# Weight conversions beside the first attention units are queued behind the exponentials of their unit, and the copies of transposes and outputs are ranked higher

## Chip, core and metric

The kernel runs on one core of a Trainium2 chip. The metric is the device time of one launch in microseconds: the median over several executions. One execution was also taken with the hardware profiler; all rows below come from it.

## What is computed

The reference, cut to what matters: a windowed attention with sink columns over 2 batches and 8 heads of 64, and then two feed-forward layers of width 2048 over the 1536 tokens.

```
scores = scale * q @ k.T                      # (2, 8, 768, 768)
keep   = (pos < n_sink) | (0 <= rel < window) # n_sink 4, window 128
a      = softmax(where(keep, scores, -1e9))
x      = (a @ v) as 1536 x 512
h = x @ w_in  (512 x 2048);  g = relu(h)**2;  x = g @ w_out (2048 x 512)
h = x @ w_in2;  P = a0 + a1*h + a2*h^2 + a3*h^3
Q = 1 + |b0|*|h| + |b1|*h^2;  g = P/(Q + 1e-6);  out = g @ w_out2
```

## The kernel before

**Groups and units.** The tokens are cut into four groups (`GROUPS`): 512, 256, 256 and 512 tokens. The attention of a group consists of units, one for each pair of heads and each segment of two blocks of 128 tokens. Group 0 has eight units, called 0 to 7 here. Even ones hold the first two blocks of the batch (score widths 128 and 256), odd ones blocks 2 and 3 (width 288 with the sink columns). A unit (`att_unit`) runs in these steps: scores on TensorE into PSUM banks (L300); on VectorE (DVE) mask and row minimum (L306); on ScalarE (ACT) the exponential with its sum (L308); on DVE one over the sum (L311, L312); normalisation of the first block on GpSimd (POOL) and of the second on DVE (L316); transposes of the normalised probabilities on TensorE (L333); their copies to SBUF, `pT` of head 0 on ACT and of head 1 on DVE (L335); in odd units also the copy `pS` of the sink columns on ACT (L347); the products with v (L356, L368); and the output, `xhi` on ACT (L374) and `xlo` on DVE (L375).

**Conversions.** Weights come as 64-bit floats. One conversion (`wconv`, which calls `w_split`) takes one block of 128x512 from a staging buffer `st` (three buffers): ACT casts `top` (L133), DVE joins it with the middle bits into `wt` (L134), ACT rounds `whi` (L419), DVE subtracts `wlo` (L420). It then asks for the next `st` load on SP's queue (L124). Conversions are numbered from 1 here, in the order of the list `lq`. Numbers 1 to 4 are the w_in blocks f = 0 to 3, 5 is w_out block 0, 6 is w_in block 4, 7 is w_out block 1, and then w_in and w_out blocks alternate.

**The loop of group 0.** In `run`, iteration k of the first loop traces the scores, exponentials and normalisation of unit k, then the transposes and copies of unit k-1, then `CONV[k]` conversions, then (for k = 3, 5, 7) six matmuls of the first layer for blocks f = 0 and 1 (`gemm1_part`, L435 to L437), then the products with v and the output of unit k-1. After the loop the first layer of group 0 runs over all 16 blocks f: `gemm1` (L435 to L437), `act1` on ACT (L444 to L446) and DVE (`glo`, L447), `gemm2a` (L458, L459, L464). Between them stand slots in which the units of group 1 advance (`tick`), and further conversions.

**What sets the order.** TensorE's order in these parts is the order in which the code is written (`manual_schedule`). The other engines and SP's queue are ordered by the framework's scheduler at build time, by priority and its own timeline; on the chip every engine then runs its list from front to back. `tc.issue_after(ins)` puts an instruction behind `ins` on its engine; `tc.high_priority(offset=...)` raises the priority of what is traced inside. `lastV` and `lastA` are the latest mask step and exponential traced by `att_unit`.

Of the kernel before, what the change touches and what calls it, by code (L numbers as in the profile page):

```python
# [37 lines left out]
YEVAC_ACT = (0, 1)  # L38
PINNED = (0, 1, 2)
NUNIT = (4, 4, 8)  # L40
CONV = (1, 1, 1, 1, 1, 1, 1, 1, 1)
PER = 5
HEAD = 2
DEPTH = 4
# [2 lines left out]
LAG2 = 3  # L47
TAIL = 3
HP = 60
NTOP = 1  # L50
IAD = 3
ST_T = 5
# [9 lines left out]
def seg_dims(seg):  # L62

    _, blk0, nb = seg
    pv = 1 if blk0 > 0 else 0
    wk = 2 * nb * P + NSK if pv else nb * P
    wq = nb * P
    nkb = nb + pv  # L70
    return wk, wq, nkb, nkb * P, (2 * nb * D if pv else 0)
# [55 lines left out]
def to_f32(nc, st, t, top):  # L127

    mid = st.bitcast(I32)[:, 1 : 1 + 2 * WH].rearrange("p (n w) -> p n w", w=2)[:, :, 0]
    head = st.bitcast(BF16)[:, 4 : 4 + 4 * WH].rearrange("p (n w) -> p n w", w=4)[:, :, 0]
    nc.scalar.copy(top.bitcast(F16).rearrange("p (n w) -> p n w", w=2)[:, :, 1], head)  # L133
    nc.vector.scalar_tensor_tensor(t.bitcast(I32), in0=mid, scalar=13, in1=top,  # L134
                                   op0=ALU.logical_shift_right, op1=ALU.bitwise_or)
# [20 lines left out]
class Fast:  # L156
# [17 lines left out]
    def setup(self):  # L174
        nc, c = self.nc, self.const
        self.zero = c.tile([P, P], BF16, name="zero")
        nc.gpsimd.memset(self.zero, 0.0)
        self.tops = [c.tile([P, WH], I32, name=f"top{i}") for i in range(NTOP)]
        self.conv_i = 0
# [231 lines left out]
    def w_split_(self, which, f, half):  # L411
        nc = self.nc
        st = self.wst.pop((which, f, half))
        t = self.stage.tile([P, WH], F32, tag="wt", name="wt", bufs=2)
        to_f32(nc, st, t, self.tops[self.conv_i % NTOP])
        self.conv_i += 1
# [83 lines left out]
    def run(self, ctx):  # L500
        tc, nc = self.tc, self.nc
# [25 lines left out]
        for u in us:  # L527
            self.att_off[u] = off
            wk, wq, _, wv, wsk = seg_dims(u[2])
# [5 lines left out]
        def prefetch():  # L535
            nonlocal nload
            if nload < len(us):
                g0 = us[nload][0] == 0
                early = (None, 0, 1, 2)[nload % DEPTH] if g0 else None
                u, alt = us[nload], nload % NALT if g0 else 0  # L540
                raws = [self.att_load(u, early, alt), None, None]
                if g0:
                    raws[1] = self.att_load_v(u, alt, 0)
                    if seg_dims(u[2])[4]:
                        raws[2] = self.att_load_v(u, alt, 1)
                loaded.append((u, raws))
                nload += 1
# [7 lines left out]
        def tick():  # L555
            with ExitStack() as c:
                if urgent:
                    c.enter_context(tc.high_priority(offset=HP))
                tick_()
            self.va_hist.append((self.lastV, self.lastA))  # L560

        def tick_():
            nonlocal done, tick_no, ui
            if tick_no % PER == 0 and loaded:
                u, raws = loaded.pop(0)
                g = u[0]
                if g not in self.x32 and g > 0:
                    self.new_x32(g)
                a = self.att_unit(u, raws, ui % NALT if g == 0 else 0)
                ui += 1  # L570
                next(a)
                new = True
            else:
                new = False
            for b in list(active)[::-1]:
                if next(b, "end") == "end":
                    active.remove(b)
                    done += 1
            if new:
                active.append(a)  # L580
                if not loaded:
                    prefetch()
            tick_no += 1
# [15 lines left out]
        cq = [list(lq[0]), list(lq[1])]  # L599
        lq0 = [(f, k) for _, f, k in lq[0]]  # L600

        def wload(which, k=1):
            for _ in range(k):
                if lq[which]:
                    self.w_load(*lq[which].pop(0))

        def wconv(which, f, half):
            if (which, f, half) in self.w:
                return
            assert cq[which].pop(0) == (which, f, half)  # L610
            self.w_split(which, f, half)
            wload(which)
# [14 lines left out]
        g0 = [None] * (n0 + 1)  # L627
        with tc.manual_schedule(engines={mybir.EngineType.PE}):
            for k in range(n0 + 1):
                if k == 0:  # L630
                    wload(0, 3)
                if k < n0:
                    u, raws = loaded.pop(0)
                    g0[k] = self.att_unit(u, raws, k % NALT)
                    for _ in range(3):
                        next(g0[k])
                if k:
                    next(g0[k - 1])
                for _ in range(CONV[k]):
                    wconv(*cq[0][0])  # L640
                while k >= 2 and pc < (k - 1) // per:
                    for f in range(HEAD):
                        self.gemm1_part(0, f, pc, self.x[0], GN[0], hb[f])
                    pc += 1
                if k:
                    next(g0[k - 1])
                while nload < n0 and len(loaded) < DEPTH - 1 or not loaded:
                    prefetch()
            done = n0
# [369 lines left out]
```

## Time and profile before

| | |
|---|---|
| median of 3 runs | 667.8 us (667.75 to 669.43) |
| the profiled execution's own time | 668.77 us |
| its span in the trace | 667.0 us |
| TensorE busy in the span | 632.6 us (95%) |
| DVE, ACT, POOL busy | 423.0, 428.4, 110.6 us |
| bytes moved by DMA | 52.39 MB |

The span is the stretch from the first to the last record; the time of the execution is 1.8 us longer. Busy time of TensorE counts matmuls as the profile models them. Times below are microseconds from the start of the span, unless marked ns.

### The profile page before, as it was taken

To read this page: it belongs to the slowest core of one execution; us is meant where nothing else is said; L and a number is where in the kernel's file an instruction comes from. 1 tells how busy PE (TensorE), PEld (TensorE's weight loads), DVE (VectorE), ACT (ScalarE), POOL (GpSimd) and SP (SyncE) were. 2 spreads that over 40 slices of the span, in tenths; PEclk is the share of its full clock that TensorE was granted. 3 is DMA by queue.
4 is the path that set the end of the run, shared out by engine and by line. 5 is a ranking of instruction groups with operands and counts; after the bars stand their busy time and mean duration, and the time that the engine had idled before them with its cause. 6 is when DMAs were issued, how large, how long until landed. Compare 5 with 4: busy or idle time off the path is not lost.

```text
span 667.0 us, 9984 instructions
## 1 busy us (share of the span) xinstructions
PE 632.6 (95%) x3681; PEld 514.7 (77%) x3681; DVE 423.0 (63%) x849; ACT 428.4 (64%) x912; POOL 110.6 (17%) x122
## 2 busy tenths in 40 slices
PE   5678999999999999999999999999999999999994
PEld 2455667777888878899888888888888888888883
DVE  5864687543333444415566649999788887877771
ACT  4854787665545555536677758778686666766661
POOL 2111010000000011103000002354233332222221
PEclk9879999999999999999999999999999999999998
DMA  7940376432111222100556620000010000100001
GB/s 285 316 163 1 130 229 200 161 118 88 34 49 50 70 67 79 31 9 14 172 194 194 195 85 2 0 1 0 1 64 0 1 0 1 57 7 2 0 1 68
DMA packets 20794, 52.39 MB, mean 79 GB/s; under 512 B 2688, under 2 KB 8064, under 8 KB 20736
## 3 DMA queue, kind: packets, MB, share of 16 engines
q1 hardware_dynamic: 20160, 51.52, 23.4%
q8 instruction: 31, 0.51, 0.3%
q14 instruction: 27, 0.22, 0.1%
q10 hardware_dynamic: 576, 0.14, 0.1%
HBM read 48.50 MB, written 3.15 MB: 77 GB/s over the span
## 4 chain that ended last, share of the span: by engine, by line
PE 89%; ACT 4%; DVE 3%; issue 1%; DMA 1%; POOL 0%; POOLq 0%; DVEq 0%
PE b L435 13%; PE b L436 13%; PE b L437 13%; PE b L458 7%; PE b L464 7%; PE b L496 7%; PE b L497 7%; PE b L495 7%; PE b L459 6%; PE b L300 3%; PE b L368 3%; PE b L333 2%; ACT p L308 2%; PE b L356 1%; DVE wt L134 1%
## 5 line engine op out<-in xcount | busy, mean ns | idle before, releaser
L435 PE MATMUL b<-xhi,whi 128*128 128x512 f32 (+1 forms) x320 | 113.4, 355 | 0.5 <-ACT xhi L374 0.5
L437 PE MATMUL b<-xhi,wlo 128*128 128x512 f32 (+1 forms) x320 | 111.0, 347 | 0.0
L436 PE MATMUL b<-xlo,whi 128*128 128x512 f32 (+1 forms) x320 | 110.9, 347 | 0.0
L458 PE MATMUL b<-ghi,whi 128*128 128x512 f32 (+1 forms) x256 | 84.9, 348 | 0.7 <-ACT ghi L445 0.7
L459 PE MATMUL b<-ghi,wlo 128*128 128x512 f32 (+1 forms) x256 | 81.9, 336 | 0.0
L486 POOL TENSOR_TENSOR glo<-t,ghi 128x512 fp32r<-128x512 f32 x34 | 45.0, 1323 | 213.3 <-ACT ghi L485 195.3
L496 PE MATMUL b<-wlo,ghi 128*128 128x512 f32 x192 | 74.7, 389 | 0.0
L495 PE MATMUL b<-whi,ghi 128*128 128x512 f32 x192 | 74.4, 389 | 0.0
L447 DVE TENSOR_TENSOR glo<-b,ghi 128x512 fp32r<-128x512 f32 (+1 forms) x64 | 35.6, 557 | 59.5 <-ACT b L446 58.9
L497 PE MATMUL b<-whi,glo 128*128 128x512 f32 x192 | 71.9, 389 | 0.0
L306 DVE CUSTOM_DVE_ANT_0 p<-b,m 128x288 f32<-128x288 f32 (+2 forms) x96 | 37.0, 419 | 54.7 <-PE b L300 54.7
L435 PEld LDWEIGHTS b<-xhi,whi 128*128 128x128 f32 x320 | 60.3, 189 | 11.9 <-issue 3.8
L308 ACT ACTIVATE p<-p,mn 128x288 f32<-128x288 f32 (+2 forms) x96 | 48.0, 501 | 33.4 <-DVE mn L306 32.9
L316 POOL TENSOR_SCALAR p<-p,sums 128x288 f32<-128x288 f32 (+1 forms) x48 | 27.1, 576 | 253.4 <-DVE sums L312 191.1
L437 PEld LDWEIGHTS b<-xhi,wlo 128*128 128x128 f32 x320 | 60.4, 189 | 7.6
L436 PEld LDWEIGHTS b<-xlo,whi 128*128 128x128 f32 x320 | 60.5, 189 | 7.3
L420 DVE TENSOR_TENSOR wlo<-wt,whi 128x512 fp32r<-128x512 f32 x64 | 45.0, 703 | 27.6 <-ACT whi L419 27.3
L419 ACT CAST whi<-wt 128x512 fp32r<-128x512 f32 x64 | 39.6, 618 | 34.5 <-PE b L436 20.9
L458 PEld LDWEIGHTS b<-ghi,whi 128*128 128x128 f32 x256 | 48.4, 189 | 12.5 <-issue 6.3
L444 ACT ACTIVATE b<-b 128x512 f32<-128x512 f32 (+1 forms) x64 | 31.0, 486 | 41.1 <-PE b L437 41.1
L464 PE MATMUL b<-glo,whi 128*128 128x512 f32 (+1 forms) x256 | 56.6, 343 | 0.0
L134 DVE SCALAR_TENSOR_TENSOR wt<-st,top 128x512 int32<-128x512 int32 x64 | 47.4, 741 | 7.5 <-ACT top L133 5.7
(126 smaller groups left out, 1287.9 us busy)
## 6 DMA issues: line engine op xcount, KB each, us to landing
st<-w SPq DMA_DIRECT2D x64, 512.0 KB, 4.1
raw<-att SPq DMA_DIRECT2D x12, 400.0 KB, 3.3
rawv<-att SPq DMA_DIRECT2D x16, 192.0 KB, 2.9
raws<-att SPq DMA_DIRECT2D x16, 128.0 KB, 2.0
out<-o SPq DMA_DIRECT2D x8, 256.0 KB, 2.0
raw_e<-att SPq DMA_DIRECT2D x4, 400.0 KB, 5.5
raw<-att SPq DMA_DIRECT2D x6, 256.0 KB, 3.4
rawv<-att SPq DMA_DIRECT2D x8, 128.0 KB, 3.9
```

Source lines behind the costliest of these rows:

```text
L134: nc.vector.scalar_tensor_tensor(t.bitcast(I32), in0=mid, scalar=13, in1=top, op0=ALU.logical_shift_right, op1=ALU.bitwise_or)
L308: self.lastA = A.activation(p, p, AF.Exp, scale=-1.0, bias=mn, accum_out=sums[:, k * nb + i : k * nb + i + 1])
L420: nc.vector.tensor_tensor(wlo, t, whi.bitcast(F32), op=ALU.subtract)
L435: nc.tensor.matmul(h[:, :n], whi[:, cs], xhi[:, c, :n], start=(c == 0), stop=False)
L436: nc.tensor.matmul(h[:, :n], whi[:, cs], xlo[:, c, :n], start=False, stop=False)
L437: nc.tensor.matmul(h[:, :n], wlo[:, cs], xhi[:, c, :n], start=False, stop=(c == NC - 1))
L458: nc.tensor.matmul(acc[m], whi[:, ms], ghi, start=(f == 0 and not pk), stop=pk, **kw)
L459: nc.tensor.matmul(acc[m], wlo[:, ms], ghi, start=False, stop=pk, **kw)
L464: nc.tensor.matmul(acc[m], whi[:, ms], glo, start=False, stop=pk or f == NF - 1, **kw)
L495: nc.tensor.matmul(acc[t], ghi[:, ts_], whi, start=(f == 0), stop=False)
L496: nc.tensor.matmul(acc[t], ghi[:, ts_], wlo, start=False, stop=False)
L497: nc.tensor.matmul(acc[t], glo[:, ts_], whi, start=False, stop=(f == NF - 1))
```

## The change

`CONV` holds the number of conversions of iterations 0 to 8. Seven instead of nine are traced in the loop, the two others follow later in the list. They are traced at the end of the iteration, after the output of unit k-1, and each of their instructions is queued behind the mask step or the exponential last traced on its engine, which is that of unit k. The transposes, copies, products with v and outputs of unit k-1 are traced with the priority raised by `HP0`. In the changed kernel the lines of these functions have a number that is one higher (L308 becomes L309).

```
-CONV = (1, 1, 1, 1, 1, 1, 1, 1, 1)
+CONV = (1, 1, 0, 1, 0, 1, 0, 1, 2)
...
+HP0 = 120
...
                 if k:
-                    next(g0[k - 1])
-                for _ in range(CONV[k]):
-                    wconv(*cq[0][0])
+                    with tc.high_priority(offset=HP0):
+                        next(g0[k - 1])
                 while k >= 2 and pc < (k - 1) // per:
                     for f in range(HEAD):
                         self.gemm1_part(0, f, pc, self.x[0], GN[0], hb[f])
                     pc += 1
                 if k:
-                    next(g0[k - 1])
+                    with tc.high_priority(offset=HP0):
+                        next(g0[k - 1])
+                with ExitStack() as cc:
+                    cc.enter_context(tc.issue_after(self.lastV.ins))
+                    cc.enter_context(tc.issue_after(self.lastA.ins))
+                    for _ in range(CONV[k]):
+                        wconv(*cq[0][0])
```

The order of instructions on TensorE and POOL is the same in both kernels; on ACT, DVE and SP's queue it differs up to the end of the first layer of group 0. Three places follow.

The first is ACT's list in the kernel before, from the third conversion to the output of unit 1; the exponentials (L308) of widths 128 and 256 are those of unit 2, `pT`, `pS` and `xhi` belong to unit 1.

```order
L133 CAST top_102<-st 128x512
L308 ACTIVATE p,sums<-p,mn 128x128 x2
L419 CAST whi<-wt 128x512
L308 ACTIVATE p,sums<-p,mn 128x256 x2
L335 COPY pT_289<-b_284 128x512
L133 CAST top_102<-st 128x512
L347 COPY pS<-b_298 128x256
L419 CAST whi<-wt 128x512
L133 CAST top_102<-st 128x512
L419 CAST whi<-wt 128x512
L133 CAST top_102<-st 128x512
L374 CAST xhi<-b_298 128x256
```

This is the same place on ACT in the changed kernel, down to the third conversion's first cast.

```order
L309 ACTIVATE p,sums<-p,mn 128x128 x2
L309 ACTIVATE p,sums<-p,mn 128x256 x2
L336 COPY pT_289<-b_284 128x512
L348 COPY pS<-b_298 128x256
L375 CAST xhi<-b_298 128x256
L309 ACTIVATE p,sums<-p,mn 128x288 x4
L134 CAST top_102<-st 128x512
```

Four `top` and three `whi` casts that stood ahead of the output of unit 1 are gone from there; the first one now follows the exponentials of unit 3.

The second place is DVE's list in the kernel before, from the last mask step of unit 3 (`b_343`) to the first of unit 4 (`b_398`); `pT_368` is unit 2's.

```order
L306 ISA p,mn<-b_343,m_127 128x288
L306 ISA mn 128x1
L420 TENSOR_TENSOR wlo<-wt,whi 128x512
L134 SCALAR_TENSOR_TENSOR wt<-st,top_102 128x512
L335 COPY pT_368<-b_364 128x384
L311 TENSOR_SCALAR sums<-sums 128x4
L312 RECIPROCAL sums<-sums 128x4
L316 TENSOR_SCALAR p<-p,sums 128x288 x2
L420 TENSOR_TENSOR wlo<-wt,whi 128x512
L134 SCALAR_TENSOR_TENSOR wt<-st,top_102 128x512
L420 TENSOR_TENSOR wlo<-wt,whi 128x512
L306 ISA p,mn<-b_398,m_125 128x128
```

In the changed kernel the same stretch of DVE runs from `b_334` to `b_389`, and unit 2's output (`xlo`) is shown behind it.

```order
L307 ISA p,mn<-b_334,m_127 128x288
L307 ISA mn 128x1
L312 TENSOR_SCALAR sums<-sums 128x4
L313 RECIPROCAL sums<-sums 128x4
L336 COPY pT_359<-b_355 128x384
L317 TENSOR_SCALAR p<-p,sums 128x288 x2
L135 SCALAR_TENSOR_TENSOR wt<-st,top_102 128x512
L421 TENSOR_TENSOR wlo<-wt,whi 128x512
L307 ISA p,mn<-b_389,m_125 128x128
L307 ISA mn 128x1
L376 TENSOR_TENSOR xlo<-b_361,xhi 128x256
```

One whole conversion (the third) stands there in place of parts of three, between unit 3's normalisation and unit 4's first mask step.

The third place is ACT's list in the kernel before at the start of the first layer: `xhi` of unit 7, then the activations of the blocks f = 0, 1 and 2 (`b_149`, `b_150`, `b_725`), then the exponentials of the first unit of group 1 and the tenth conversion.

```order
L374 CAST xhi<-b_678 128x256
L444 ACTIVATE b_149<-b_149 128x512
L444 ACTIVATE b_150<-b_150 128x512
L445 ACTIVATE ghi<-b_149 128x512
L446 ACTIVATE b_149<-b_149 128x512
L444 ACTIVATE b_725<-b_725 128x512
L445 ACTIVATE ghi<-b_150 128x512
L446 ACTIVATE b_150<-b_150 128x512
L445 ACTIVATE ghi<-b_725 128x512
L446 ACTIVATE b_725<-b_725 128x512
L308 ACTIVATE p,sums<-p,mn 128x288 x2
L133 CAST top_102<-st 128x512
```

The same start on ACT in the changed kernel; the casts are those of the conversions 7, 8 and 9.

```order
L375 CAST xhi<-b_651 128x256
L420 CAST whi<-wt 128x512
L134 CAST top_102<-st 128x512
L445 ACTIVATE b_149<-b_149 128x512
L445 ACTIVATE b_150<-b_150 128x512
L446 ACTIVATE ghi<-b_149 128x512
L447 ACTIVATE b_149<-b_149 128x512
L420 CAST whi<-wt 128x512
L134 CAST top_102<-st 128x512
L445 ACTIVATE b_725<-b_725 128x512
L446 ACTIVATE ghi<-b_150 128x512
L447 ACTIVATE b_150<-b_150 128x512
```

In the stretch behind it, ahead of the exponentials of group 1's first unit, `whi` of conversion 9 and all of conversion 10 follow, so that ten conversions stand ahead of those exponentials instead of nine. The conversions 4, 5 and 6 stand behind the exponentials of the units 5 and 7 and around the copies of unit 7.

## Rows read from the trace of the kernel before

**Rows 1.** Busy time by stretch; columns as in its header.

```profile
core 0: us, PE busy (x) PEld busy (x) DVE busy (x) ACT busy (x) POOL busy (x), PEclk, DMA share, GB/s
...
16.30:43.10 26.80, 17.56 (x132) 12.03 (x132) 21.61 (x61) 19.34 (x49) 3.44 (x7) 0.75 0.82 288
43.10:63.50 20.40, 17.07 (x160) 11.77 (x158) 11.62 (x45) 10.65 (x35) 3.04 (x6) 1.00 0.08 21
...
92.00:150.00 58.00, 58.00 (x332) 43.54 (x333) 35.66 (x82) 41.51 (x90) 4.90 (x6) 1.00 0.52 170
```

**Rows 2.** Timeline of TensorE, 16 to 44 us; waits in brackets.

```profile
22.34 1.04 PE L356 MATMUL b<-pS,raws 128*64 128x128 f32 x8 [2.71 <-ACT pS L347]
23.17 1.92 PE L368 MATMUL b<-pT,rawv 128*64 128x128 f32 x12
25.02 1.60 PE L300 MATMUL b<-raw_e 64*64 64x288 f32 x16
28.07 0.84 PE L333 MATMUL b<-ident,p 128*128 128x128 f32 x6 [1.45 <-DVE xlo L375]
...
32.25 1.13 PE L368 MATMUL b<-pT,rawv 128*64 128x256 f32 x8 [1.94 <-ACT pT L335]
...
37.55 1.94 PE L333 MATMUL b<-ident,p 128*128 128x128 f32 x8 [2.68 <-DVE xlo L375]
...
43.08 1.20 PE L300 MATMUL b<-raw_e 64*64 64x288 f32 x16
```

**Rows 3.** Timeline of ACT, 16 to 30 us.

```profile
21.94 0.35 ACT L347 COPY pS<-b 128x256 f32<-128x256 f32 x1
...
23.66 0.77 ACT L133 CAST top<-st 128x512 f16<-128x512 bf16 x1
...
25.71 0.78 ACT L133 CAST top<-st 128x512 f16<-128x512 bf16 x1
```

**Rows 4.** Groups by line over the whole span: the four steps of a conversion.

```profile
L133 ACT CAST top<-st 128x512 f16<-128x512 bf16 x64 | 49.5, 774 | 1.2 <-DVE wt L134 1.2
...
L134 DVE SCALAR_TENSOR_TENSOR wt<-st,top 128x512 int32<-128x512 int32 x64 | 47.4, 741 | 7.5 <-ACT top L133 5.7
L420 DVE TENSOR_TENSOR wlo<-wt,whi 128x512 fp32r<-128x512 f32 x64 | 45.0, 703 | 27.6 <-ACT whi L419 27.3
L419 ACT CAST whi<-wt 128x512 fp32r<-128x512 f32 x64 | 39.6, 618 | 34.5 <-PE b L436 20.9 <-DVE wt L134 13.5
```

**Rows 5.** Busy time by stretch, cut where the granted clock changes.

```profile
22.90:26.10 3.20, 3.20 (x30) 2.10 (x30) 1.83 (x4) 2.20 (x4) 0.00 (x0) 0.53 0.57 186
...
33.10:43.20 10.10, 6.96 (x54) 4.89 (x54) 6.59 (x20) 5.31 (x16) 1.85 (x3) 0.51 0.67 238
43.40:63.50 20.10, 16.77 (x158) 11.56 (x150) 11.62 (x45) 10.45 (x35) 3.04 (x6) 1.00 0.08 21
```

**Rows 6.** Timeline of all engines, 42 to 58 us.

```profile
46.01 0.46 ACT L335 COPY pT<-b 128x384 f32<-128x384 f32 x1
...
46.52 0.87 PE L368 MATMUL b<-pT,rawv 128*64 128x256 f32 x8
...
48.27 0.27 DVE L306 CUSTOM_DVE_ANT_0 p<-b,m 128x128 f32<-128x128 f32 x1
...
49.04 1.06 PE L333 MATMUL b<-ident,p 128*128 128x128 f32 x8 [0.83 <-DVE xlo L375]
...
52.85 1.20 PE L300 MATMUL b<-raw_e 64*64 64x288 f32 x16
```

**Rows 7.** Timeline of ACT, 57 to 72 us.

```profile
63.02 0.37 ACT L374 CAST xhi<-b 128x256 fp32r<-128x256 f32 x1 [3.13 <-PE b L368]
64.90 1.07 ACT L444 ACTIVATE b<-b 128x512 f32<-128x512 f32 x2 [1.51 <-PE b L437]
...
71.59 0.54 ACT L308 ACTIVATE p<-p,mn 128x288 f32<-128x288 f32 x1 [2.14 <-DVE mn L306]
```

**Rows 8.** Timeline of TensorE, 57 to 93 us.

```profile
70.23 0.72 PE L300 MATMUL b<-raw 64*64 64x288 f32 x8 [1.60 <-DVE glo L447]
...
90.28 0.70 PE L300 MATMUL b<-raw 64*64 64x288 f32 x4 [1.03 <-DVE mn L306]
```

## The prediction, made before the changed kernel ran

> **What bounds the kernel now.** I first cut the span into stretches by busy time [rows 1]. From 92 us on, as far as that table goes, TensorE is busy without a gap (58.00 of 58.00 us), and TensorE's share over the whole span is 95%. Its order is unchanged, so what the change can win must come from the beginning, where TensorE waits: in 16.3 to 43.1 us it is busy for 17.56 of 26.80 us, and in 43.1 to 63.5 for 17.07 of 20.40 [rows 1]. Every microsecond by which the first layer starts earlier is then handed on to the end, because nothing behind it but TensorE's own work decides.
>
> Next I read TensorE's timeline in the worse stretch [rows 2]. Four waits stand there: 2.71 us for `pS` of unit 1, 1.45 for its `xlo`, 1.94 for `pT` of unit 2, 2.68 for the `xlo` of unit 2, together 8.8. All are for small attention results of ACT and DVE. (Transposes wait for an `xlo` because they take over the PSUM bank that it reads.) ACT's list shows what stands ahead of these results: casts of conversions, which come every 2.05 us (23.66 and 25.71) [rows 3]. That is the period of a chain that goes back and forth: `top` 0.77 us on ACT, `wt` 0.74 on DVE, `whi` 0.62 on ACT, with `wlo` 0.70 on DVE beside the next one [rows 4]. Each step waits for the other engine, and attention queued behind it waits as well. Nine conversions are done before 38 us, none between there and the start of the first layer.
>
> So this trace holds both cases. The scores of the odd units 3, 5 and 7 begin at 25.02, 43.08 [rows 2] and 52.85 [rows 6]. With conversions in between, a pair of units takes 18.06 us; without, 9.77. The clock takes part: it is at the 1.2 GHz level from 22.9 to 26.1 and from 33.1 to 43.2 (granted 0.53 and 0.51), and at 2.4 GHz from 43.4 to 63.5, where TensorE is busy for 16.77 of 20.10 us [rows 5]. Ahead of each fall TensorE had mostly waited.
>
> **The change, part by part.** I work in stages, each ending at the scores of an odd unit; times are estimates from the rows.
>
> A, to the scores of unit 3. Conversion 2 stays where it is. Ahead of `pS` of unit 1 two `top` casts and one `whi` go: 2 x 0.77 + 0.62 = 2.2 us of ACT [rows 4]. Not all of it comes through: DVE's copy of unit 1's transposes is needed too, and it now stands behind unit 2's normalisation, in place of behind two half conversions. I let the products with `pT` start at 21.7 instead of 23.17 [rows 2], so 1.5 us (bounds 1.0 and 2.2). They took 1.92 us at half clock; at full clock I estimate half of that, which saves another 0.9 (bounds 0 and 0.9). Sum 2.4, and unit 3's scores start at 22.6.
>
> B, from unit 3's scores to unit 5's. The base is the pair without conversions, 9.77 us, at full clock. In it the next even unit's first mask step comes 48.27 - 43.08 = 5.19 us after the scores [rows 2, 6]. Conversion 3 is added, and by DVE's list it stands whole between unit 3's normalisation and unit 4's first mask step: `wt`, wait for `whi`, `wlo` is 0.74 + 0.62 + 0.70 = 2.06 us [rows 4]. Against it, `pT` of unit 2 (0.46 us, [rows 6]) no longer sits between the exponentials, so the normalisation comes about 0.4 earlier. Unit 4's mask steps, the `xlo` of unit 2 and with it unit 3's transposes are thus late by 1.7 us. The first cast, `top` (0.77), and the fourth exponential delay `pT` of unit 2 and hence its products with v (46.52 in the row) by about a microsecond; this lies inside the 1.7. Estimate 11.5 us instead of 18.06: 6.6 won. Bounds: 9.8 if the conversion is hidden, 14 if the clock falls again; so 4.1 to 8.3.
>
> C, from unit 5's scores to unit 7's. Conversion 4 is split: only `wt` (0.74) stands ahead of unit 6's mask steps, `wlo` ahead of the last of them. Unit 5's transposes had 0.83 us of wait [rows 6], all for the `xlo` that `wt` now delays, but `pS` of unit 5 moves ahead of the last exponential. I take 0.4 lost (bounds 0 and 1.4, the two steps of DVE).
>
> D, unit 7 to the first activation. Conversions 5, 6 and 7 and the first cast of 8 come here. ACT has idle time for them: 3.13 us ahead of `xhi` of unit 7 and 1.51 ahead of the first activation [rows 7]. `whi` 7 and `top` 8 need 0.62 + 0.77 = 1.39, under 1.51. Cost 0; if that cover were gone it would be 1.4.
>
> E, start of the first layer. `whi` 8 and `top` 9 now stand between the activations of f = 0 and f = 2. The next scores wait for `glo` of f = 2, since they take its bank (1.60 us in 70.23's row, [rows 8]), so this delay is on TensorE's path: I take 1.2 of the 1.39 us (bounds 0 and 2.8, two pairs of casts). The casts behind (`whi` 9, conversion 10) fall in ACT's next gap of 2.14 us [rows 7].
>
> F, until TensorE runs without gaps. Once conversion 10 is through, the list is one conversion ahead of the one before, and the later 1.03 us of wait at 90.28 [rows 8] may go or double. I take 0 (plus or minus 1).
>
> Loads: an `st` load waits until its buffer's conversion has been read, three conversions ahead. The DMA engines are nearly idle from 43.1 to 63.5 (21 GB/s [rows 1]). In the changed order the loads from the seventh on follow the conversions 4, 5, ..., several microseconds before they are read. I cost SP's new order at nothing; the units' own loads move earlier past the `st` loads. The raised priority costs nothing either, and gains only what is counted above.
>
> Sum: 2.4 + 6.6 - 0.4 - 0 - 1.2 + 0 = 7.4 us. The profiled execution took 668.77 us, which becomes 661.4. It lies 0.97 us above the median of the runs shown, so for the median: 667.8 - 7.4 = **660.4 us**.
>
> One rule is weighed here. The rows show the clock at the lower level for 13 us, each time after TensorE had waited much [rows 5]. The Trainium skill ("TensorE: Matmul & The Clock Gate", part 1) says that half rate is the array's default and that only activity releases it. That speaks against counting on full clock in A and B, because the changed stretch still has waits of over a microsecond. By my rows the sum is 7.4 us; by the rule read strictly it would be about 4 (first rival).
>
> **Rivals.**
>
> 1. The clock stays low in A and B. Place: the waits that stage B still has, for `pT` of unit 2 and for unit 4's late mask steps. Price: 0.9 in A and 2.5 in B (11.5 becomes 14): 7.4 - 3.4 = 4.0, so 663.8. For it: TensorE fell twice there before. Against it: it held the upper level from 43.4 to 63.5 with waits of 0.83 [rows 5, 6], and conversion 3 adds only 1.7 us.
>
> 2. The conversions are only moved: the first layer needs 5, 6, 7, 4 in turn, and if TensorE waits there for whole conversions, each exposed one costs 2.05 us [rows 3]. Of 5 to 10, three exposed ones take 6.2 of 7.4 us: 666.6, within the noise. From 3.6 exposed ones on, the kernel is slower than before; with all six it is 12.3 us, thus 672.7. For it: ACT and DVE are the busier ones at that start. Against it: conversion 5 is done some 6 us and 7 some 10 us before their matmuls, by D.
>
> 3. Conversions 3 and 4 hide entirely and the later waits vanish: stage B takes 9.8, C costs 0, E about 0, F gains 1. Then 2.4 + 8.3 + 1 = 11.7, so 656.1. For it: in the pair without conversions DVE is busy 11.62 of 20.40 us [rows 1], so there is room. Against it: DVE's list puts conversion 3 exactly where unit 4 waits.
>
> 4. The change does not do what it says: the scheduler leaves the lists as they were, and the time is 667.8. The lists differ as shown, so this gets next to nothing.
>
> **How the numbers follow.** My own case (gains of 5.5 to 9.5, 658.3 to 662.3) gets 0.58; rival 1 (gains of 2 to 5.5) 0.17; rival 3 (over 9.5) 0.10; rival 2 within 2.0 us of no change, 0.08, and slower 0.06; rival 4, 0.01. About 0.3%, or 2.0 us, is what a measurement of this kernel tells from no change. Faster: 0.58 + 0.17 + 0.10 = 0.85; same 0.08 + 0.01 = 0.09; slower 0.06. The range takes most of rivals 1 and 3: 657.4 to 665.4. The likeliest case's own range is 658.3 to 662.3.
>
> **What would show it.** In the changed profile unit 3's scores should begin near 22.6 us, unit 5's near 34, unit 7's near 44, the first activation near 56.5; granted clock 1.00 from 22 to 44; TensorE's waits for `pS` and `xlo` of units 1 and 2 each under 1.5 us. The scores of group 1's first unit should wait for `glo` some 1.2 us longer than 1.60. I would be wrong if the first activation comes before 53 or after 60, if a `top` cast waits for an `st` load, or if TensorE has gaps beyond about 85 us that it did not have.

## The result, and the profile after

| | before | after |
|---|---|---|
| median | 667.77 us (667.14 to 669.43, 4 runs) | 661.66 us (660.90 to 663.49, 4 runs) |
| ratio, 95% interval | | 0.9904 [0.9882, 0.9927] |
| profiled execution, its span | 668.77, 667.0 us | 663.49, 661.6 us |
| mean granted clock of the profiled execution | 0.985 | 0.989 |

The kernel became 6.1 us faster; 660.4 was forecast, with 657.4 to 665.4 as the range. The profiled execution is the slowest of the four; the others took 660.90, 661.15 and 662.17 us at a mean granted clock of 0.996, 0.994 and 0.993. That matters below.

TensorE's timeline of the changed kernel, answering [rows 2, 6, 8]:

```profile
20.94 0.66 PE L357 MATMUL b<-pS,raws 128*64 128x128 f32 x8 [1.36 <-ACT pS L348]
...
23.00 1.20 PE L301 MATMUL b<-raw_e 64*64 64x288 f32 x16
...
27.58 0.87 PE L369 MATMUL b<-pT,rawv 128*64 128x256 f32 x8 [1.18 <-ACT pT L336]
...
31.01 1.06 PE L334 MATMUL b<-ident,p 128*128 128x128 f32 x8 [1.75 <-DVE xlo L376]
...
33.38 1.12 PE L357 MATMUL b<-pS,raws 128*64 128x128 f32 x8 [1.08 <-ACT pS L348]
...
36.13 2.20 PE L301 MATMUL b<-raw_e 64*64 64x288 f32 x16
...
46.69 1.20 PE L301 MATMUL b<-raw_e 64*64 64x288 f32 x16
...
51.86 0.66 PE L334 MATMUL b<-ident,p 128*128 128x128 f32 x4 [0.85 <-POOL p L317]
52.90 0.66 PE L334 MATMUL b<-ident,p 128*128 128x128 f32 x4 [0.39 <-POOL p L317]
...
65.80 0.71 PE L301 MATMUL b<-raw 64*64 64x288 f32 x8 [2.80 <-DVE glo L448]
```

The scores of the units 3, 5 and 7 now begin at 23.00, 36.13 and 46.69 us. They began at 25.02, 43.08 [rows 2] and 52.85 [rows 6]. Of the four long waits of [rows 2] the one for the `xlo` of unit 1 is gone, and the others are 1.36, 1.18 and 1.75. The wait for `glo` is 2.80 in place of 1.60 [rows 8].

Busy time by stretch of the changed kernel, in the columns of [rows 1] (so the seventh is the granted clock). The first three stretches are the stages B, C and D of the prediction, the next two are cut where the granted clock is low:

```profile
23.00:36.13 13.13, 9.12 (x83) 6.20 (x83) 8.19 (x30) 7.14 (x23) 1.84 (x4) 0.86 0.48 143
36.13:46.69 10.56, 9.26 (x84) 6.08 (x83) 8.06 (x30) 7.09 (x23) 2.03 (x3) 0.85 0.29 90
46.69:59.26 12.57, 10.82 (x83) 7.67 (x82) 9.42 (x25) 8.70 (x21) 2.05 (x4) 1.00 0.30 95
32.80:39.50 6.70, 6.12 (x43) 4.09 (x44) 3.20 (x14) 2.38 (x10) 0.81 (x2) 0.51 0.26 83
67.20:70.40 3.20, 3.20 (x9) 2.49 (x9) 1.82 (x6) 2.44 (x7) 0.00 (x0) 0.55 0.56 164
92.00:150.00 58.00, 58.00 (x337) 43.79 (x336) 34.04 (x76) 40.53 (x88) 4.29 (x7) 1.00 0.51 171
```

The clock is at the 1.2 GHz level from about 32.5 to 39.3 and from 66.6 to 70.1 us. The first fall lies across the end of B and the start of C; it comes after the waits of 1.18 and 1.75 and inside that of 1.08. From 92 to 150 us TensorE is busy without a gap, as before [rows 1].

DVE's timeline shows what makes the wait of 1.75:

```profile
28.27 0.67 DVE L135 SCALAR_TENSOR_TENSOR wt<-st,top 128x512 int32<-128x512 int32 x1
29.63 0.69 DVE L421 TENSOR_TENSOR wlo<-wt,whi 128x512 fp32r<-128x512 f32 x1 [0.68 <-ACT whi L420]
30.24 0.28 DVE L307 CUSTOM_DVE_ANT_0 p<-b,m 128x128 f32<-128x128 f32 x1
...
30.45 0.42 DVE L376 TENSOR_TENSOR xlo<-b,xhi 128x256 fp32r<-128x256 f32 x1
...
51.88 0.67 DVE L135 SCALAR_TENSOR_TENSOR wt<-st,top 128x512 int32<-128x512 int32 x1
```

Conversion 3 occupies DVE's list from 28.27 to 30.24, its wait for `whi` included. Only then come unit 4's mask step and unit 2's `xlo`. (The last row is taken up at the end.)

ACT's timeline at the start of the first layer, answering [rows 7]:

```profile
59.26 1.07 ACT L445 ACTIVATE b<-b 128x512 f32<-128x512 f32 x2 [0.31 <-PE b L438]
...
61.22 0.63 ACT L420 CAST whi<-wt 128x512 fp32r<-128x512 f32 x1
61.73 0.80 ACT L134 CAST top<-st 128x512 f16<-128x512 bf16 x1
62.37 0.65 ACT L445 ACTIVATE b<-b 128x512 f32<-128x512 f32 x1
```

The first activation starts at 59.26 instead of 64.90 [rows 7]. The two casts at 61.22 and 61.73 push the activation of f = 2 back to 62.37, and `glo` with it.

One count from ahead of the prediction has to be set right. In the kernel before, ACT's trace has this row:

```profile
35.23 0.76 ACT L133 CAST top<-st 128x512 f16<-128x512 bf16 x1
```

It is the tenth `top` cast; the next one comes at 72.64. So ten conversions, not nine, stand in the first stretch of the kernel before, the cast shown there behind the exponentials of group 1 belongs to the eleventh, and ten stand ahead of those exponentials in both kernels.

### The profile page after: what moved, and what is told of

The parts are those of the page before. It is cut to its first block, busy times and chain, and to the rows that moved or that the text cites. A ratio compares the mean times of both kernels' runs of the same rounds, so it can differ in the third digit from the quotient of the medians.

```text
span 661.6 us, 9984 instructions
## 1 busy us (share of the span) xinstructions
PE 630.8 (95%) x3681; PEld 514.0 (78%) x3681; DVE 423.3 (64%) x849; ACT 427.8 (65%) x912; POOL 111.4 (17%) x122
## 4 chain that ended last, share of the span: by engine, by line
PE 90%; ACT 4%; DVE 2%; DMA 2%; issue 1%; POOL 0%; SPq 0%; POOLq 0%; ACTq 0%
PE b L436 14%; PE b L437 13%; PE b L438 13%; PE b L459 7%; PE b L465 7%; PE b L497 7%; PE b L498 7%; PE b L460 7%; PE b L496 7%; PE b L301 3%; PE b L369 3%; PE b L334 2%; PE b L357 1%; ACT p L309 1%; DMA raw_e<-att 1%; DMA st<-w 1%
## 5 line engine op out<-in xcount | busy, mean ns | idle before, releaser
L309 ACT ACTIVATE p<-p,mn 128x288 f32<-128x288 f32 (+2 forms) x96 | 48.0, 501 | 33.3 <-DVE mn L307 32.9
L420 ACT CAST whi<-wt 128x512 fp32r<-128x512 f32 x64 | 39.5, 618 | 32.8 <-PE b L437 20.9
L445 ACT ACTIVATE b<-b 128x512 f32<-128x512 f32 (+1 forms) x64 | 31.0, 486 | 39.5 <-PE b L438 39.3
L460 PEld LDWEIGHTS b<-ghi,wlo 128*128 128x128 f32 x256 | 48.5, 189 | 4.7
```

What stands on the lines that cost most here:

```text
L309: self.lastA = A.activation(p, p, AF.Exp, scale=-1.0, bias=mn, accum_out=sums[:, k * nb + i : k * nb + i + 1])
L460: nc.tensor.matmul(acc[m], wlo[:, ms], ghi, start=False, stop=pk, **kw)
```

## The experiments

Main theory: the queued casts of the conversions delayed the attention results, and their new places decide each stage. Rival: the clock is the main cause, and the casts matter little. Each ratio is to the kernel before, timed on the same chip.

**The changed kernel once more.**

> The changed kernel once more, on the chip of the runs beside it, as their measure. 0.990 of the kernel before (0.987 to 0.993). If the low clock in stage B is a matter of the execution and not of the program, its profile may show stage B near 11.8 us instead of 13.1.

662.70 us (662.02 to 663.80, 5 runs), 0.9919 [0.9906, 0.9932]. Its profiled execution (662.02 us, clock 0.995) has no fall of the clock in the stages B and C:

```profile
23.52:35.37 11.85, 7.81 (x84) 5.30 (x83) 8.20 (x30) 7.15 (x23) 1.86 (x4) 1.00 0.46 149
35.37:45.41 10.04, 7.82 (x85) 5.30 (x83) 7.80 (x30) 6.95 (x23) 2.03 (x3) 1.00 0.35 106
```

The lists are the same, and the waits in B nearly so: 1.21 for unit 2's `pT`, 1.75 for its `xlo`, 1.08 for unit 3's `pS`. Without the fall B takes 11.85 instead of 13.13 and C 10.04 instead of 10.56: the low clock cost 1.8 us in the first profile. It comes in some executions and not in others.

**Conversions 3 and 4 later, out of B and C.**

```
-CONV = (1, 1, 0, 1, 0, 1, 0, 1, 2)
+CONV = (1, 1, 0, 0, 0, 0, 0, 0, 5)
```

> The changed kernel with no conversion in the iterations 2 to 7 and five in the last one: CONV = (1, 1, 0, 0, 0, 0, 0, 0, 5). The conversions 3 to 7 then all stand behind the exponentials of unit 7. By my theory (a conversion costs what it holds up in the lists of ACT and DVE ahead of attention results) stage B becomes the pair without conversions: scores of unit 3 at 23.0 us, of unit 5 near 33, of unit 7 near 43, against 36.1 and 46.7 in the changed kernel. The last stage gets longer, since conversion 3 is needed for the first layer's block f = 2 right behind unit 7's transposes: I let it grow from 12.6 to 14 us. First activation near 57, median near 659.5 (658 to 661). By the rival that conversions are only moved and come back whole at the first layer, two conversions more there cost 4 us: first activation near 59 or later, median 661.5 to 664.

661.34 us (660.45 to 663.34, 5 runs), 0.9891 [0.9873, 0.9909]. The stages B and C:

```profile
22.89:33.33 10.44, 8.32 (x83) 5.47 (x83) 7.00 (x28) 6.00 (x21) 1.86 (x4) 1.00 0.39 117
33.33:43.11 9.78, 7.83 (x84) 5.30 (x83) 6.88 (x28) 6.02 (x21) 1.93 (x4) 1.00 0.20 55
```

C without a conversion is 9.78, the 9.77 of the prediction's base pair. B without one is 10.44, so conversion 3 costs 11.85 - 10.44 = 1.4 and the part of conversion 4 in C 10.04 - 9.78 = 0.3. Together 1.7 us are won in B and C. From unit 7's scores (43.11) to group 1's (63.75) it takes 20.64 us, against 19.11 in the repeated profile: 1.5 are given back, among it a new wait of 0.45 for the `wlo` of a conversion and one of 0.86 for `xhi`, which is 0.47 in both profiles of the changed kernel. Right behind group 1's scores the clock falls:

```profile
63.90:67.30 3.40, 3.40 (x14) 2.06 (x12) 3.05 (x8) 2.64 (x8) 0.00 (x0) 0.50 0.47 184
```

A conversion taken out of the first units has to be paid for later; the ratio is not clearly below that of the changed kernel.

**All nine conversions in the loop, each behind the exponentials of its unit.** The waits alone, with the old counts and, at both calls of `next(g0[k - 1])`, the old priority.

```
-CONV = (1, 1, 0, 1, 0, 1, 0, 1, 2)
+CONV = (1, 1, 1, 1, 1, 1, 1, 1, 1)
...
                 if k:
-                    with tc.high_priority(offset=HP0):
+                    if True:
                         next(g0[k - 1])
```

> The waits behind the unit's exponentials, but one conversion in every iteration as in the kernel before, and no raised priority. Conversions 3 to 9 are then spread over the units 1 to 7 and none stands between the first activations. By my theory each conversion inside the units costs up to 1.7 us and the cast ahead of unit 1's copies 0.5 in stage A; stages A to C together lose 1 to 3 us against the changed kernel, the wait for glo at the first layer falls from 2.80 to about 1.6. Median near 662.5 (661 to 664.5). By the rival that the first layer's start is what matters and conversions inside the units are free: 660.5.

665.49 us (664.83 to 665.58, 5 runs), 0.9944 [0.9930, 0.9957], above what I had expected. TensorE in its stage B:

```profile
31.77 1.06 PE L334 MATMUL b<-ident,p 128*128 128x128 f32 x8 [1.74 <-DVE xlo L376]
...
34.75 1.12 PE L357 MATMUL b<-pS,raws 128*64 128x128 f32 x8 [1.70 <-ACT pS L348]
35.66 1.92 PE L369 MATMUL b<-pT,rawv 128*64 128x128 f32 x12
37.51 2.20 PE L301 MATMUL b<-raw_e 64*64 64x288 f32 x16
```

Units 3, 5, 7 start at 23.76, 37.51 and 48.09, `glo`'s wait is 1.59 again, and the later waits for `mn` return (0.90 and 0.28). B takes 13.75 us instead of 18.06, partly at the low clock, but the two are not the same work: with the waits two conversions stand in B, before it was about six. The fair measure is the start of group 1's scores. Ten conversions are done ahead of that group's exponentials in both, and its scores start at 66.14 instead of 70.23 [rows 8]. The waits alone bring 3.5 us (668.99 to 665.49), the whole change about 6; the rest needs the lower counts as well.

**The raised priority alone,** on the kernel before, at both calls.

```
                 if k:
-                    next(g0[k - 1])
+                    with tc.high_priority(offset=120):
+                        next(g0[k - 1])
```

> The kernel before with the raised priority alone: no waits, one conversion in each iteration. The scheduler gives the same lists of instructions on all engines as for the kernel before, so this is also a measure of the noise. 1.000 of the kernel before, 0.998 to 1.002. If the raised priority did anything on the chip that the lists do not show, it would be faster than that.

668.38 us (667.26 to 669.47, 11 runs), 0.9995 [0.9986, 1.0004]: nothing. The lists of all engines are those of the kernel before, and the changed kernel without the raised priority has the changed kernel's lists. This half of the change does nothing here. The new counts alone, without the waits, leave ACT's, DVE's and SP's order as it was, too: the waits act by themselves, the counts only together with them.

**Two conversions in stage B.**

```
-CONV = (1, 1, 0, 1, 0, 1, 0, 1, 2)
+CONV = (1, 1, 0, 2, 0, 0, 0, 1, 2)
```

> The changed kernel with the conversions 3 and 4 both behind the exponentials of unit 3, none beside the units 4 to 6: CONV = (1, 1, 0, 2, 0, 0, 0, 1, 2). By my theory the price of a conversion depends on its place: another wt, and the casts, ahead of unit 4's mask steps and copies cost 1 to 2 us more in stage B (13 to 14 us at full clock), and stage C is back at 9.8; in all 0.5 to 1.5 us slower than the changed kernel. If only the number of conversions beside the units counts, it is the same as the changed kernel.

664.52 us (663.09 to 665.91, 6 runs), 0.9938 [0.9923, 0.9953], 1.8 us above the changed kernel on the same chip. The wait for `xlo` grew from 1.75 to 2.43:

```profile
31.86 1.77 PE L334 MATMUL b<-ident,p 128*128 128x128 f32 x8 [2.43 <-DVE xlo L376]
...
34.70 1.12 PE L357 MATMUL b<-pS,raws 128*64 128x128 f32 x8 [0.64 <-ACT pS L348]
...
37.46 1.88 PE L301 MATMUL b<-raw_e 64*64 64x288 f32 x16
```

B takes 14.29, with its end at the low clock. From 34.70 to unit 5's scores it takes 2.76 us, where the repeated profile takes 1.46 (33.91 to 35.37) for the same work at full clock; so B at full clock is about 13.0, an estimate, which lies at the lower end of what was expected. The direction is the theory's. The 1.8 us between the medians, more than expected, is not the place alone: in this profile the clock fell a second time, behind group 1's scores, which it did not in the repeated one.

```profile
66.20:73.00 6.80, 6.14 (x20) 4.22 (x21) 4.98 (x11) 4.80 (x10) 0.00 (x0) 0.50 0.42 151
```

**Extra matmuls in the changed kernel,** to hold the clock. Eight matmuls of zeros into an unused PSUM bank ahead of and behind the transposes of the iterations 2 to 6; the function:

```
+        def spin():
+            for _ in range(8):
+                nc.tensor.matmul(idle[:, :P], self.zero, self.zero, start=True, stop=True,
+                                 skip_group_check=True)
```

> The changed kernel with eight small matmuls of zeros into an unused PSUM bank ahead of and behind the transposes in the iterations 2 to 6, so that TensorE is active while it would wait; they write nothing that is read. If the granted clock is what made stage B 13.1 instead of 11.5 us, the clock stays at 1.00 from 23 to 45 us, the scores of unit 5 start near 34.6 instead of 36.1, and the median is near 660.3 (659.5 to 661). If the lists of ACT and DVE alone set the pace, the low clock costs nothing, and the dummies are paid where TensorE does not wait (about 0.5 us a place): 662 to 664.

664.29 us (664.00 to 665.64, 5 runs), 0.9931 [0.9917, 0.9944]. The clock part came out: 1.00 in B and C, which take 11.11 and 11.12. The time did not:

```profile
23.07:34.18 11.11, 9.72 (x115) 7.14 (x114) 8.23 (x30) 7.15 (x23) 2.23 (x4) 1.00 0.49 157
34.18:45.30 11.12, 9.73 (x117) 7.15 (x115) 8.22 (x30) 7.15 (x23) 2.23 (x4) 1.00 0.32 96
88.20:91.50 3.30, 3.30 (x10) 2.59 (x10) 3.00 (x10) 3.30 (x9) 0.46 (x1) 0.61 0.77 249
```

The first layer starts 1.4 us earlier than in the first profile after, but only 0.15 earlier than in the repeated one, where the clock stayed up by itself; C is 1.1 longer than there. And much later stand a wait and a fall of the clock (third row) that the changed kernel does not have:

```profile
86.00 0.70 PE L301 MATMUL b<-raw 64*64 64x288 f32 x4 [2.60 <-DVE mn L307]
```

The scheduler had moved some of ACT's casts as well, so this run does not price the clock by itself.

**The same matmuls in the kernel before.** This is the rival's test: with the clock held, the old order should be nearly as fast.

> The kernel before with the same dummy matmuls as in the earlier run, so that TensorE's clock has a reason to stay up while the casts stay in the lists; the scheduler moves some casts on ACT by a place or two. If the low clock was the main loss (a rival to my theory), the stretch from the scores of unit 3 to those of unit 5 falls from 18.06 to 13 us or less and most of the gain of the change is there: 662 to 664. If the queued casts are the main loss, the stretch stays at 15 us or more and the median is above 665.

666.21 us (664.85 to 667.49, 6 runs), 0.9963 [0.9950, 0.9976]. From 24 to 36 us the clock is now up:

```profile
24.00:36.00 12.00, 8.51 (x94) 6.23 (x93) 11.32 (x34) 10.68 (x30) 1.64 (x2) 0.99 0.89 302
36.00:43.00 7.00, 5.60 (x47) 3.35 (x45) 4.79 (x14) 3.30 (x8) 0.83 (x2) 0.53 0.68 224
```

Even so TensorE still waits 3.01 us for an `xlo` there, and B takes 40.61 - 24.00 = 16.61 us, against 18.06 [rows 2] before and 11.85 in the changed kernel. DVE is busy 11.32 of 12.00 us: the conversions fill it. The clock falls again inside B, and by the 1.3 us that this cost in the changed kernel B at full clock would be about 15.3, an estimate. So the casts are the main cause and the clock adds to it: the extra matmuls bring 2.4 us (668.60 to 666.21) of the change's 6. (Some casts moved as well, so this is not the price of the clock by itself.)

**Conversions of the first layer's start queued behind the activations of f = 2.**

```
-        nc.scalar.activation(r, r, AF.Square)
+        self.lastA1 = nc.scalar.activation(r, r, AF.Square)
...
+        held = []
...
-                if g == 0 and f + 4 < NF:
+                if g == 0 and f == 2:
+                    with ExitStack() as cd:
+                        cd.enter_context(tc.issue_after(self.lastA1.ins))
+                        for z in held:
+                            wconv(*z)
+                        wconv(0, f + 4, 0)
+                elif g == 0 and f < 2:
+                    held.append((0, f + 4, 0))
+                elif g == 0 and f + 4 < NF:
                     wconv(0, f + 4, 0)
...
-                if g == 0 and f + 1 < NF:
+                if g == 0 and f < 2:
+                    held.append((0, f + 1, 1))
+                elif g == 0 and f + 1 < NF:
                     wconv(0, f + 1, 1)
```

> The changed kernel, with the conversions 8 to 11 of the first layer queued behind the last activation of f = 2. This prices stage E alone. By my theory the wait for glo of f = 2 falls from 2.80 to about 1.6 us, and the clock does not fall behind it (it was low from about 67 to 70.5 us); the conversions are two casts later, so a wait of up to 1 us may come back near 85 us. Median near 660.5 (659.5 to 662). If the casts between the activations cost nothing: 661.7.

661.19 us (660.77 to 662.59, 4 runs), 0.9886 [0.9869, 0.9904]. Group 1's scores:

```profile
63.08 0.71 PE L301 MATMUL b<-raw 64*64 64x288 f32 x8 [1.59 <-DVE glo L448]
```

The wait for `glo` is 1.59 again, 1.2 less, as term E has it. Later waits of 0.80 and 0.28 for `mn` return, and the span is only 0.6 us shorter than in the repeated profile (659.6 to 660.2), so in the trace most of it is given back.

**Both joined:** `CONV = (1, 1, 0, 0, 0, 0, 0, 0, 5)` and the deferred conversions.

> Both edits that gained: no conversion in the iterations 2 to 7, and the conversions of f = 0 to 2 of the first layer queued behind the last activation of f = 2. If the gains of stage B and of stage E add up: scores of unit 5 near 33.3 us, wait for glo near 1.6 instead of 2.75, median 2 to 3 us below the changed kernel. If the conversions now come too late for the first layer, waits for wlo or whi appear at the blocks f = 2 to 4 or the scores of group 1 wait for mask steps by over 2 us, and the median is that of the changed kernel.

659.11 us (658.91 to 660.64, 4 runs), 0.9868 [0.9852, 0.9883], 3.6 us below the changed kernel on the same chip (662.70): faster than both kernels.

```profile
33.42 1.20 PE L301 MATMUL b<-raw_e 64*64 64x288 f32 x16
...
43.21 1.20 PE L301 MATMUL b<-raw_e 64*64 64x288 f32 x16
...
63.20 0.72 PE L301 MATMUL b<-raw 64*64 64x288 f32 x8 [2.10 <-DVE glo L448]
```

B and C take 10.45 and 9.79, `glo` is waited for 2.10, and neither a fall of the clock nor a later wait stands up to 92 us. Its span is 3.1 us shorter than that of the repeated profile (657.1 to 660.2). Of these, 1.3 stand at group 1's scores (63.20 to 64.52), and 0.55 of them already at unit 3's (22.97 to 23.52), where the lists are still the same. By 122 us the lead of the same DVE instructions has grown to 2.4, and it stays there up to 649 us; the last 0.7 come in the last ten microseconds. What made the 1.0 us between 64 and 122 is open.

**The third conversion ahead, with the deferred ones:** `CONV = (1, 2, 0, 0, 0, 0, 0, 0, 4)`.

> As the run that joins the two gains, with conversion 3 taken out of the last stage and put behind the exponentials of unit 1: CONV = (1, 2, 0, 0, 0, 0, 0, 0, 4). Its casts then stand ahead of unit 1's copies. By my theory stage A gets 0.5 to 1 us longer (scores of unit 3 at 23.5 to 24), stages B and C stay at 10.4 and 9.8, and the last stage gets back what conversion 3 cost there (the wait of 0.45 for wlo and 0.4 more for xhi, and half a microsecond of the wait for glo): 658.5 to 659.5, that is the same within the noise. If the last stage is bound by the number of conversions still to be done, it gains 2 us: 657.

661.68 us (661.17 to 661.91, 4 runs), 0.9902 [0.9887, 0.9917], above what I had expected.

```profile
21.57 1.12 PE L357 MATMUL b<-pS,raws 128*64 128x128 f32 x8 [2.74 <-ACT pS L348]
22.48 1.92 PE L369 MATMUL b<-pT,rawv 128*64 128x128 f32 x12
24.33 2.20 PE L301 MATMUL b<-raw_e 64*64 64x288 f32 x16
```

The additional casts ahead of unit 1's copies raised the wait for `pS` from 1.68 (the joined version) to 2.74; the products with `pT` run at the low level (1.92, as in [rows 2]), and unit 3's scores begin 1.4 us later. The last stage gave 1.1 of it back, as expected, the 0.45 us wait for `wlo` among it: group 1's scores begin at 63.48, only 0.3 later than in the joined version. The larger part of the loss lies behind, where the clock is at the low level (0.50):

```profile
65.00:68.40 3.40, 3.40 (x10) 2.66 (x9) 2.72 (x6) 2.71 (x7) 0.00 (x0) 0.50 0.67 230
```

At 72 us the same DVE instructions are 1.8 us later than in the joined version, from 122 us on 2.3. The joined version, with the same wait for `glo` (2.10; here 2.09), has no such fall. So this run shows what the third conversion costs in stage A, but most of what it lost in its profile comes with a fall of the clock that the expectation left out.

## Why the prediction was right, and which term was off

**The mechanism held.** The waits that went are those for attention results behind casts. Adding a conversion in B lengthened it, removing it shortened it, and holding the clock up in the old order for most of B brought 2.4 of the 6 us. The terms, in the profiled execution after, against 7.4 us:

| term | predicted | measured | from |
|---|---|---|---|
| A, to unit 3's scores | 2.4 | 2.0 | 25.02 - 23.00 |
| B, unit 3 to 5 | 6.6 | 4.9 | 18.06 - 13.13 |
| C, unit 5 to 7 | -0.4 | -0.8 | 9.77 - 10.56 |
| D, unit 7 to first activation | 0 | -0.5 | 12.05 - 12.57 |
| E, wait for `glo` | -1.2 | -1.2 | 1.60 - 2.80 |
| sum | 7.4 | 4.4 | 70.23 - 65.80 |
| F, behind it | 0 | 1.0 | span 5.4 shorter - 4.4 |

**The mis-sized term is B:** "Estimate 11.5 us instead of 18.06: 6.6 won". It took 13.13, and three parts of it are measured. The base was 10.44, not 9.77: in the new lists unit 2's `pT` stands behind all four exponentials of unit 3 even where no conversion is near, in the pair that I took as base it stands ahead of the fourth. I had named this delay and held it to lie inside the 1.7. Conversion 3 added 1.4 (I had 1.7). The low clock added 13.13 - 11.85 = 1.3. Without it, 11.85 stands 0.35 above the estimate, because the two errors of size partly cancel.

**The clock.** "Granted clock 1.00 from 22 to 44" was wrong for this execution and right for the repeated one. Rival 1 therefore happened in part: it priced the low clock in B at 2.5; it cost 1.3, and 0.5 in C. The rule of the Trainium skill weighed in the prediction ("TensorE: Matmul & The Clock Gate", part 1: only activity releases half rate) fits the profile with its 0.51 from 32.8 to 39.5 us. That its total of about 4 is near the 4.4 of that profile is chance: the low clock cost 1.8 there and not 3.4, and the other terms made up the rest. The repeated profile, with nearly the same waits, kept 1.00 and gained 70.23 - 64.52 = 5.7. So a fall in B is one outcome among several of the same program.

**The other marks.** Unit 3 near 22.6 was 23.00 (ten of unit 1's products with `pT` waited once more, 0.18 us at 21.99, for DVE's copy); unit 5 near 34 was 36.13 (35.37 repeated); unit 7 near 44 was 46.69 (45.41). The first activation near 56.5 was 59.26 (57.98), inside the bound of 60. "Waits for `pS` and `xlo` of units 1 and 2 each under 1.5" failed for unit 2's `xlo` (1.75): the cause is conversion 3 in DVE's list, which I had named. Unit 1's `pS` held it in the first profile (1.36) and not in the repeated one (1.62). No `top` cast waited for a load, and no gap beyond 85 us came: the waits of 1.03 [rows 8] and 0.28 us for `mn` went. F had been left at 0 "plus or minus 1". Its reason, a list one conversion ahead, was wrong, since ten conversions stand ahead of group 1's exponentials in both kernels. Nor is a microsecond at group 1's scores simply handed on: the first profile's lead over the kernel before grows from 4.4 us there to 5.5 by 126 us, and only from then on it stays.

**Rivals 2 to 4.** No conversion was exposed as a whole at the first layer; what E cost is one pair of casts. Conversion 3 was not hidden (rival 3). The lists did change (rival 4), though not by the priority.

**The total came out nearer than its terms.** The profile after gained 5.4 us in span and the medians 6.1, since the median execution has more of the full clock than the profiled one. Nearly right in sum thus means B too large by 1.7, C and D by 0.9 together and A by 0.4, against F too small by 1.0 and a profiled execution with less of the full clock than the median one. That the median lies within 1.3 us of the forecast is therefore in part luck.

**What stays open.** Why the waits for `mn` near 86 us come in some lists (before, nine conversions, deferred alone, extra matmuls in both kernels) and not in others (changed, joined) was seen, not controlled; the same holds for the fall of the clock behind group 1's scores, which came in the first profile after and in three experiments; none of these runs changes that place alone. What the clock alone is worth in the old order was not isolated either, because the extra matmuls also moved casts.

## What to carry to other kernels

Where in-order engines feed the one that bounds the kernel, the place of side work in their lists counts beside its amount: with ten conversions ahead of group 1's exponentials in either order, its scores began at 70.23 us or, with the conversions spread behind the exponentials of their units, at 66.14. Per piece the crowded place was not dearer: B held about six conversions before, and (15.3 - 10.44) / 6 is about 0.8 us each, an estimate, against 1.4 for the single one. They were crowded into one stage while the later stages had idle time. Compare the built lists first, since they show which half of a change moves anything at all; the priority moved nothing. Side work that is pushed out comes back later (1.7 us won and 1.5 given back with the conversions 3 and 4 moved), so move it until no place has a wait for it, and leave room for a clock that differs from execution to execution.

## What I had not expected of the hardware

**The same program at different clocks.** Mean granted clock and time of the changed kernel's nine runs go from 0.996 and 660.90 us to 0.989 and 663.80. In the two profiles nearly the same waits led to a fall in one and to none in the other, worth 1.8 us over B and C (23.69 to 21.89).

**POOL slows beside DVE.** Unit 7's normalisation on POOL, in the kernel before:

```profile
57.38 1.11 POOL L316 TENSOR_SCALAR p<-p,sums 128x288 f32<-128x288 f32 x2 [4.87 <-DVE sums L312]
```

and in the changed kernel:

```profile
51.22 1.63 POOL L317 TENSOR_SCALAR p<-p,sums 128x288 f32<-128x288 f32 x2 [4.11 <-DVE sums L313]
```

These take 0.52 us longer where DVE's step `wt` (0.67 us from 51.88) starts before they end. This is the -0.5 of term D: unit 7's transposes wait a second time, 0.39 us at 52.90. The repeated profile has 1.64. The kernel before shows the same beside DVE's step `wlo`, in unit 3's normalisation:

```profile
32.50 1.64 POOL L316 TENSOR_SCALAR p<-p,sums 128x288 f32<-128x288 f32 x2 [10.13 <-DVE sums L312]
...
33.17 0.67 DVE L420 TENSOR_TENSOR wlo<-wt,whi 128x512 fp32r<-128x512 f32 x1
```

In both, the second of the two POOL instructions takes 1.07 us instead of 0.55. Beside `xlo`, one of whose inputs is in PSUM, it takes 0.55 (unit 7 in the kernel before). The Trainium skill ("SBUF — State Buffer", rules for kernel authors) says that of a DVE instruction with two SBUF inputs and a GpSimd one that reads SBUF, the second to issue blocks until the first is done. `wt` and `wlo` have two inputs in SBUF, and the added 0.52 is less than their 0.67, so that one of the two blocks agrees with the traces. Which one does not follow from the records: POOL's starts 0.10 us ahead of `wt`, and yet it is POOL's that gets longer. No run took `wt` away alone.
